# Reordering the start of a gated-recurrence and MLP kernel: later loads, the first transposed y on another queue, and a third unit begun in another order

## The chip, the cores and the metric

The kernel runs on one core of a Trainium2 chip. A core has five engines with an instruction stream each: TensorE (PE, matmuls and transposes), VectorE (DVE), ScalarE (ACT), GpSimd (POOL) and SyncE (SP), which here only issues DMAs. The metric is device time in microseconds, the median of several executions. Before the change it is 630.16 us (3 runs, 629.78 to 631.45).

## The reference

```python
f = 1.0 / (1.0 + np.exp(-f_logit))            # all of (4, 8, 768, 48)
for t in range(S):
    state = f[:, :, t, :, None] * state + np.einsum('bhd,bhe->bhde', k[:, :, t], v[:, :, t])
    y[:, :, t] = np.einsum('bhd,bhde->bhe', q[:, :, t], state)
x = y.transpose(0, 2, 1, 3).reshape(B * S, H * D)      # 3072 tokens, 384 columns
h = x @ w_in                                           # w_in 384 x 2048
g = h * (1.0 / (1.0 + np.exp(-1.702 * h)))
out = g @ w_out                                        # w_out 2048 x 384
```

A gated linear recurrence over 768 tokens for 4 batches and 8 heads, and behind it an MLP over all tokens. All data are float32.

## The kernel before

**Units.** The tokens are cut into 12 units of 256 (three for each batch). `attention(n)` builds one unit as a list of parts; each part is a function that issues instructions. The recurrence inside a chunk of 64 tokens is done by six levels (block sizes 1 to 32). At each level TensorE makes scores (`sc`, L392) from q and a copy of k set aside by ScalarE (`Kc`, L448; in units from the fourth on also a copy of q, `Qc`, L454). VectorE multiplies q and k by products of gates (`promote`: L473 in two halves for the first three units, L477 in one piece afterwards) and puts the scores into the matrix A under masks (L421, L441). After the levels, k is turned (`tkn`, copied to `kn`), A times v gives the inner part of y (L488), k times v the change of state (L576), and VectorE chains the four chunk states (L591 to L595, eight or seven short operations in a row). Then the states times q are added to y (L616), eight copies take y out of PSUM into `yT` (L627), and six DMAs bring `yT` into `xT`, where the MLP reads it (`to_x`, L648 and L653).

**Beginning a unit.** Three functions bring f, q and k of a unit into place: `begin_f`, `begin`, `begin_k`. In the first three units TensorE transposes them (L344) and ScalarE copies them out of PSUM (L349); from the fourth unit on VectorE does it (L332). f also passes a sigmoid on ScalarE, which must load another activation table before it and the table of the MLP's gelu after it. `begin_k` ends by setting k aside and, from the fourth unit on, by the first promotion. `begin_gates` makes the products of gates on GpSimd (L383). Each begin-function also issues the next unit's DMA load of the same input into the one `raw` buffer (`load_raw`).

**The MLP.** `mlp_blocks` (units 0 to 2, cut into four blocks of ff columns) and `mlp_unit` (the others) are lists of small TensorE steps: `h` (L784: three matmuls, then gelu on ScalarE, L788, into g) and `o` (L810; in later units seven products, L761). `merge` walks through a unit's attention parts and, after each, issues MLP steps in proportion to a share by the part's kind. So TensorE's order is written out by hand; it is the merged list. On the other engines a scheduler may move instructions. The weights come in 16 pieces of 768 KB (`fetch_weights`, L199, three buffers `bits`), and each is converted by one ScalarE operation (L217) and four VectorE operations (L219 to L222), dealt out among the parts by `convert`.

**Queues.** SP issues all loads and stores in one order[...].[...]

**The order around the change.** `parts_of(n)` puts the next unit's begin-functions among the parts of unit n. For n = 0: f and q between the late levels, k at the end. For n = 1: the third unit's q with the first part, its f before the last level but one, its k at the end. For n = 2 and 3: f, then q, then k, and after k the part with unit n's states. The inter-chunk y of unit n (L616) is issued with the first part of unit n + 1.

Of the kernel before, what the change touches and what calls it, by code (L numbers as in the profile page):

```python
# [16 lines left out]
def view(t, offset, dims):  # L17

    a = t[:]
    return bass.AP(a.tensor, a.offset + offset, [list(a.ap[0])] + [list(d) for d in dims])  # L20
# [3 lines left out]
def kernel(  # L24
# [33 lines left out]
    nc = tc.nc  # L58
    B, H, S, D = q.shape
# [10 lines left out]
    HS = 64  # L70
# [6 lines left out]
    N_FILL = 3  # L77
# [24 lines left out]
    def keep_up(times, columns=384, of=None):  # L102

        if times:
            pt = ps.tile([P, columns], F32, tag="mm", name=f"idle_{next(serial)}", bufs=4)
        for _ in range(times):
            lhs, rhs = of or (ident, masks.rearrange("p l f t -> p (l f t)"))
            nc.tensor.matmul(pt, lhsT=lhs, rhs=rhs, start=True, stop=True)  # L108
# [42 lines left out]
    def query(n, f):  # L151

        return ((2, 3), (4, 5) if n < N_FILL else (0, 5))[n % 2][f]

    q_end = const.tile([P, NP], F32, name="q_end")
# [14 lines left out]
    for r in range(NGR):  # L170
        ffs = range(r * FG, (r + 1) * FG)
        for ff in ffs[::2]:
            f = slice(ff * P, (ff + 2) * P)
# [126 lines left out]
    def rows(h):  # L300
        return slice(h * HS, h * HS + D)
# [4 lines left out]
    def attention(n):  # L306
# [10 lines left out]
        t = {"tms": [F]}  # L317
        parts = []

        def part(kind):  # L320
            return lambda fn: parts.append((kind, fn))

        def slot(s):
            return X[:, s]
# [31 lines left out]

        def begin_f():
            turn(0, lambda f: F[:, ORDER.index(f) * SLOT:(ORDER.index(f) + 1) * SLOT], AF.Sigmoid)
            if n:
                load_raw(n + 1, 0)  # L360

        def begin():
            turn(1, lambda f: slot(query(n, f)))
            if n:
                load_raw(n + 1, 1)

        def begin_k():
            turn(2, lambda f: slot((KR, KF)[f]))
            if n:
                load_raw(n + 1, 2)  # L370
            if n >= N_FILL:
                set_aside(0, True)
                promote(0)
            else:
                set_aside(0)
# [31 lines left out]
        def columns(h, g):  # L407

            return rows(h ^ g)
# [188 lines left out]
        @part("W")  # L598
        def _():

            py = t["py"]
            for cs in ((1, 0), (2, 3)):
                for a in range(NP):
                    for c in cs:
                        g, f = CHUNK[c]
                        w = HS
                        if t["before"][c] is None:
                            if not n:  # L610
                                continue
                            w = 1
                        for h in range(2):
                            state = t["before"][c][rows(h), a] if w > 1 else t["ahead"][rows(h), NC - 1, a]
                            x = a * HALF + g * HS
                            nc.tensor.matmul(  # L616
                                py[columns(h, g), g, a, f, :w], lhsT=state, rhs=X[rows(h), query(n, f), x:x + w],
                                start=False, stop=True, skip_group_check=True,
                            )
            yT = att.tile([P, NP, NG, G], F32, tag="kn", name=f"yT_{n}", bufs=1)  # L620
            xT = xTs[n] = mlp.tile([P, NK, width(n)], F32, tag="xT", name=f"xT_{n}", bufs=3)
            for f in (1, 0):
                for g in range(NG):
                    for h in range(2):
                        at, step = (g * HS, 1) if f else (U - 1 - g * HS, -1)
                        copy = nc.vector.tensor_copy if n == 0 and not f else nc.scalar.copy
                        copy(view(yT[rows(h)], at, [[U, NP], [step, HS]]), py[columns(h, g), g, :, f, :])  # L627
            to_x(lambda h: (yT[rows(h), :NK], lambda r, d: yT[r:r + d, NK]), xT[:, :, :U], NG)
            if n == NALL - 1:

                pl = ps.tile([P, NP], F32, tag="mm", name="y_last", bufs=4)
                for a in range(NP):
                    for h in range(2):
                        nc.tensor.matmul(
                            pl[rows(h), a:a + 1], lhsT=last["st"][rows(h), NC - 1, a], rhs=q_end[rows(h), a:a + 1],
                            start=True, stop=True,
                        )
                yl = att.tile([P, NP], F32, tag="q_last", name="yT_last", bufs=1)
                for h in range(2):
                    nc.scalar.copy(yl[rows(h)], pl[rows(h)])  # L640
                yl = yl.rearrange("p (a g t) -> p a g t", g=1, t=1)
                to_x(lambda h: (yl[rows(h), :NK], lambda r, d: yl[r:r + d, NK]), xT[:, :, U:], 1)

        def to_x(y, x, ng):

            for h in range(2):
                most, rest = y(h)
                nc.sync.dma_start(out=x[h * D:(h + 1) * D].rearrange("p c (g t) -> p c g t", g=ng), in_=most)  # L648
                at = 0
                while at < D:  # L650
                    c, p = (h * D + at) // DR, (h * D + at) % DR
                    w = min(D - at, DR - p)
                    nc.sync.dma_start(  # L653
                        out=x[D2 + p:D2 + p + w, c].rearrange("p (g t) -> p g t", g=ng), in_=rest(h * HS + at, w)
                    )
                    at += w
# [114 lines left out]
    def width(n):  # L771

        return U + (n == NALL - 1)
# [49 lines left out]
    def mlp_unit(n):  # L823
        g = {}

        def last_token():
            po = ps.tile([P, DM], F32, tag="mm", name="o_last", bufs=4)
            nc.tensor.matmul(po[:1], lhsT=ones, rhs=g["last"][:, 0], start=True, stop=True)
            nc.scalar.copy(g["last"][:1, 0], po[:1])
            nc.sync.dma_start(out=out[NALL * U - 1:, :], in_=g["last"][:1, 0])  # L830
        o = mlp_o7(n, g)
        if width(n) > U:
            o.insert(3 * HF, (DM, last_token, 0))
        return mlp_h(n, range(NFF), g, True) + o
# [28 lines left out]
    def parts_of(n):  # L863

        parts = list(units[n][1])
        _, inter = parts.pop()
        if n:
            kind, scores = parts[0]
            _, ahead = units[n - 1][1][-1]
            parts[0] = kind, lambda: (ahead(), scores())  # L870
        if n == 0:

            def and_idle(l):
                kind, fn = parts[l]
                return kind, lambda: (fn(), keep_up(2 * (l < 3)))
            parts[:NL] = [and_idle(l) for l in range(NL)]
        if n + 1 < NALL:
            begin_f, begin, begin_k, begin_gates = units[n + 1][0]
            i = len(parts)
            if n + 1 < N_FILL:  # L880

                parts.append(("K", lambda: (begin_k(), begin_gates())))
                parts.insert(i - 4, ("B", begin if n == 0 else lambda: None))
                parts.insert(i - 5, ("B", begin_f))
                if n:

                    kind, head = parts[0]
                    parts[0] = kind, lambda: (head(), begin(), keep_up(2 * (n == 1)))
                    if n == 1:
                        second = parts[1][1]  # L890
                        parts[1] = kind, lambda: (second(), keep_up(2))
            else:
                kind, states = parts.pop()
                if n in CARRY:
                    parts += [("B", begin_f), ("B2", begin), ("S1", lambda: (states(), begin_gates())), ("K3", begin_k)]
                else:
                    parts += [("B", begin), ("B", begin_k), (kind, lambda: (states(), begin_gates()))]
                    parts.insert(i - 3, ("B", begin_f))
        else:
            parts.append(("W", inter))  # L900
        return parts
# [58 lines left out]
    load_raw(1, 2)  # L960
    fetch_weights()
    fetch_weights()
    with nc.allow_non_contiguous_dma("one token"):
        for h in range(2):
            nc.sync.dma_start(out=q_end[h * HS:h * HS + D], in_=q[B - 1, h::2, S - 1, :].rearrange("a d -> d a"))
    fill = []
    merge(0, fill, 0, steady, deal=(0, 0, 0, 0, 0, 0, 0, 4, 1, 1, 0, 0))
    fill += mlp_blocks((0, 0)) + mlp_blocks((0, 1))
# [5 lines left out]
    fill_order.close()  # L974
    for n in range(3, NALL):
        fill += mlp_unit(n)
    for n in range(4, NALL):
        merge(n, fill, NFF * NK * U + 7 * HF * HC, late, chores=list(sums_of_b()) if n == 4 else ())
    for _, emit, _ in fill:
# [30 lines left out]
```

## Time and profile before

| | |
|---|---|
| median of 3 runs | 630.16 us |
| the profiled execution | 630.85 us |
| its span, first to last instruction | 629.0 us |
| TensorE busy | 603.4 us (96%) |
| VectorE busy | 385.4 us (61%) |
| ScalarE busy | 262.4 us (42%) |
| GpSimd busy | 42.3 us (7%) |
| mean DMA rate | 93 GB/s |

The page counts an engine as busy while an instruction runs. TensorE is busy nearly always, so the span is its work plus the time it waits; and its work takes longer where the granted clock (PEclk, tenths of full speed) is low. All of this lies in the first 240 us.

### The profile page before, as it was taken

To read this page: it belongs to the slowest core of one execution; us is meant where nothing else is said; L and a number is where in the kernel's file an instruction comes from. 1 tells how busy PE (TensorE), PEld (TensorE's weight loads), DVE (VectorE), ACT (ScalarE), POOL (GpSimd) and SP (SyncE) were. 2 spreads that over 40 slices of the span, in tenths; PEclk is the share of its full clock that TensorE was granted. 3 is DMA by queue.
4 is the path that set the end of the run, shared out by engine and by line. 5 is a ranking of instruction groups with operands and counts; after the bars stand their busy time and mean duration, and the time that the engine had idled before them with its cause. 6 is when DMAs were issued, how large, how long until landed. Compare 5 with 4: busy or idle time off the path is not lost.

```text
span 629.0 us, 17072 instructions
## 1 busy us (share of the span) xinstructions
PE 603.4 (96%) x7318; PEld 519.6 (83%) x7318; DVE 385.4 (61%) x632; ACT 262.4 (42%) x546; POOL 42.3 (7%) x91
## 2 busy tenths in 40 slices
PE   6888799889999999999999999999999999999997
PEld 5566577667678688989989989989989989989896
DVE  1788866678766656667657658646758646321441
ACT  3444554453155345345355355345345344232220
POOL 3010010020001002002002002002002001000000
PEclk9988799999999999999999999999999999999999
DMA  7857863372043451452553243543151111001000
GB/s 170 209 134 163 216 159 100 85 189 70 1 104 88 132 145 49 105 153 54 126 132 70 62 125 80 129 110 86 47 154 28 47 48 28 26 2 26 25 2 25
DMA packets 83308, 58.20 MB, mean 93 GB/s; under 512 B 33633, under 2 KB 75265, under 8 KB 83233
## 3 DMA queue, kind: packets, MB, share of 16 engines
q1 hardware_dynamic: 82480, 55.94, 35.6%
q10 hardware_dynamic: 753, 1.18, 0.8%
q8 instruction: 57, 0.93, 0.6%
q14 instruction: 18, 0.15, 0.1%
HBM read 43.98 MB, written 8.39 MB: 83 GB/s over the span
## 4 chain that ended last, share of the span: by engine, by line
PE 88%; ACT 3%; DVE 3%; DMA 2%; issue 2%; SPq 1%; ACTq 0%; DVEq 0%
PE h L784 37%; PE o L810 10%; PE o_Y L761 8%; PE o_Z L761 8%; PE o_X L761 7%; PE sc L392 6%; PE o_W L761 4%; PE t L344 2%; PE y L488 2%; PE sc L576 2%; PE y L616 2%; DMA raw<-in_f_logit_dram 1%; DMA bits<-in_moe_w_in_dram 1%; PE idle L108 1%; ACT yT L627 1%
## 5 line engine op out<-in xcount | busy, mean ns | idle before, releaser
L784 PE MATMUL h<-xT,w_in 128*128 128x256 f32 (+1 forms) x1152 | 258.6, 382 | 2.1 <-ACT g L788 2.1
L784 PEld LDWEIGHTS h<-xT,w_in 128*128 128x128 f32 x1152 | 217.5, 191 | 33.9 <-ACT g L788 2.7
L788 ACT ACTIVATE g<-h 128x256 f32<-128x256 f32 (+1 forms) x192 | 72.6, 385 | 199.1 <-PE h L784 198.7
L477 DVE TENSOR_TENSOR X<-X,tot 128x1024 f32<-128x1024 f32 x45 | 55.1, 1225 | 41.5 <-PE sc L392 35.2
L448 ACT COPY Kc<-X 128x512 f32<-128x512 f32 x72 | 48.0, 667 | 47.5 <-DVE X L477 24.7
L810 PE MATMUL o<-w_out,g 128*128 128x384 f32 x192 | 67.6, 503 | 0.0
L810 PEld LDWEIGHTS o<-w_out,g 128*128 128x128 f32 x192 | 36.3, 194 | 22.8 <-issue 1.2
L761 PE MATMUL o_Y<-T,S 128*128 128x192 f32 x288 | 51.7, 329 | 0.0
L441 DVE COPY_PREDICATED A<-masks,sc 128x256 f32<-128x256 uint32 (+1 forms) x108 | 51.0, 533 | 0.3
L761 PE MATMUL o_X<-w_out,g 128*128 128x192 f32 x288 | 49.7, 326 | 0.0
L761 PEld LDWEIGHTS o_Y<-T,S 128*128 128x128 f32 x288 | 47.0, 190 | 1.1 <-issue 0.7
L761 PEld LDWEIGHTS o_X<-w_out,g 128*128 128x128 f32 x288 | 47.5, 190 | 0.5
L383 POOL TENSOR_TENSOR tot<-F 128x512 f32<-128x512 f32 x12 | 12.5, 1041 | 473.7 <-DVE st L594 425.4
L392 PE MATMUL sc<-X,Kc 48*64 48x64 f32 x1440 | 31.2, 223 | 13.4 <-ACT Kc L448 7.3
L392 PEld LDWEIGHTS sc<-X,Kc 48*64 48x64 f32 x1440 | 26.4, 137 | 20.7 <-ACT Kc L448 10.3
L332 DVE STREAM_TRANSPOSE X<-raw 128x512 f32<-128x512 f32 x36 | 37.9, 1109 | 4.3 <-PE y L616 3.8
L627 ACT COPY yT<-y 48x256 f32<-48x256 f32 x92 | 33.7, 367 | 4.9 <-PE y L616 3.7
L699 DVE TENSOR_TENSOR g<-g,g 128x512 f32<-128x512 f32 x18 | 12.4, 691 | 37.3 <-ACT g L788 37.3
L473 DVE TENSOR_TENSOR X<-X,tot 128x512 f32<-128x512 f32 x30 | 20.2, 688 | 11.8 <-PE sc L392 11.8
L383 POOL TENSOR_TENSOR tot<-tot 128x256 f32<-128x256 f32 (+4 forms) x60 | 27.0, 449 | 4.7
L761 PE MATMUL o_Z<-w_out,g 128*128 128x192 f32 x144 | 26.7, 331 | 0.0
L697 DVE TENSOR_TENSOR S<-g 128x512 f32<-128x512 f32 x18 | 12.4, 692 | 21.7 <-ACT g L788 21.4
(93 smaller groups left out, 642.6 us busy)
## 6 DMA issues: line engine op xcount, KB each, us to landing
bits<-in_moe_w_out_dram SPq DMA_DIRECT2D x8, 768.0 KB, 7.0
raw<-in_f_logit_dram SPq DMA_DIRECT2D x48, 96.0 KB, 2.3
raw<-in_k_dram SPq DMA_DIRECT2D x48, 96.0 KB, 2.5
raw<-in_q_dram SPq DMA_DIRECT2D x44, 96.0 KB, 2.3
bits<-in_moe_w_in_dram SPq DMA_DIRECT2D x7, 576.0 KB
k_tok<-z SPq DMA_DIRECT2D x56, 64.0 KB, 1.8
kt<-k_tok SPq DMA_DIRECT2D x14, 256.0 KB, 2.9
xT<-yT SPq DMA_DIRECT2D x24, 144.0 KB, 2.7
```

Of the source, the lines that this page charges most:

```text
L332: nc.vector.transpose(view(out, at, [[HALF, NP], [step, R4], [R4 * step, 32]]), by_half[:, j, f].rearrange("p a (j d) -> p (a j) d", j=R4) ...
L383: nc.gpsimd.tensor_tensor(tn, t2[:, :, 0], t2[:, :, 1], ALU.mult)
L392: nc.tensor.matmul(t["sc"][g * HS:(g + 1) * HS, h, a, s, :], lhsT=t["Kc", l][rows(h), x:x + HS], rhs=rhs(h, a, g), start=True, stop=True,)
L441: nc.vector.copy_predicated(out=view(A, at, dims), mask=mask.bitcast(U32), data=got)
L448: nc.scalar.copy(c.rearrange("p (n two m) -> p n two m", two=2, m=m), view(X, KF * SLOT, [[2 * m, SLOT // (2 * m)], [(KR - KF) * SLOT + m, ...
L473: nc.vector.tensor_tensor(x, x, y, ALU.mult)
L477: nc.vector.tensor_tensor(x, x, y, ALU.mult)
L627: copy(view(yT[rows(h)], at, [[U, NP], [step, HS]]), py[columns(h, g), g, :, f, :])
L761: nc.tensor.matmul(t[bank], lhsT=lhs(f), rhs=rhs(f), start=(new and f == 0), stop=(f == HF - 1), skip_group_check=True,)
L784: nc.tensor.matmul(ph, lhsT=w_in[:, c, ff * P:(ff + 1) * P], rhs=xTs[n][:, c, :], start=(c == 0), stop=(c == NK - 1))
L788: nc.scalar.activation(g[ff // FG][:, ff % FG, :], ph, AF.Gelu_apprx_sigmoid)
L810: nc.tensor.matmul(t["po"], lhsT=g[ff // FG][:, ff % FG, tt * P:(tt + 1) * P], rhs=w_out[:, ff, :], start=(ff == ffs[0]), stop=(ff == ffs[ ...
```

## The change

- A load of the third unit (n = 2) is issued at other places: f in unit 1's `begin_f` as before, q with the first part of unit 1, k after the third unit's q has been turned. The three loads of the fourth unit are issued together, with the second part of unit 2, not in the third unit's begin-functions.
- The load of the last token's q (`q_end`) moves from the start to a later place in the source.
- The first unit's six `xT` DMAs are issued by ScalarE, not by SP. Its eight `yT` copies are shared by rows (heads: ScalarE the even, VectorE the odd), not by direction.
- In unit 1 the third unit's f is turned before level 2, ahead of the first gelu, and its q before level 4; two of the four filling matmuls (`keep_up`) go.
- In units 2 and 3 the states of unit n come before the next unit's `begin_k`; in unit 3 the next unit's q comes right after its f.

```diff
-            if n:
+            if n >= N_FILL or (n == 1 and 0 == 0):
                 load_raw(n + 1, 0)
...
-            if n:
+            if n >= N_FILL or (n == 1 and 1 == 0):
                 load_raw(n + 1, 1)
...
-            if n:
+            if n >= N_FILL or (n == 1 and 2 == 0):
                 load_raw(n + 1, 2)
...
-                        copy = nc.vector.tensor_copy if n == 0 and not f else nc.scalar.copy
+                        copy = nc.vector.tensor_copy if n == 0 and h else nc.scalar.copy
...
+            queue = nc.sync if n else nc.scalar
...
-                nc.sync.dma_start(out=x[h * D:(h + 1) * D].rearrange("p c (g t) -> p c g t", g=ng), in_=most)
+                queue.dma_start(out=x[h * D:(h + 1) * D].rearrange("p c (g t) -> p c g t", g=ng), in_=most)
...
-                parts.insert(i - 4, ("B", begin if n == 0 else lambda: None))
-                parts.insert(i - 5, ("B", begin_f))
-                if n:
+                if n == 0:
+                    parts.insert(i - 4, ("B", begin))
+                    parts.insert(i - 5, ("B", begin_f))
+                else:
                     kind, head = parts[0]
-                    parts[0] = kind, lambda: (head(), begin(), keep_up(2 * (n == 1)))
-                    if n == 1:
-                        second = parts[1][1]
-                        parts[1] = kind, lambda: (second(), keep_up(2))
+                    parts[0] = kind, lambda: (head(), load_raw(n + 1, 1), keep_up(2))
+                    parts.insert(4, ("B", lambda: (begin(), load_raw(n + 1, 2))))
+                    parts.insert(2, ("B", begin_f))
...
+                elif n < N_FILL:
+                    second = parts[1][1]
+                    parts[1] = parts[1][0], lambda: (second(), [load_raw(n + 1, j) for j in range(3)])
+                    parts += [("B", begin), (kind, lambda: (states(), begin_gates())), ("B", begin_k)]
+                    parts.insert(i - 3, ("B", begin_f))
                 else:
-                    parts += [("B", begin), ("B", begin_k), (kind, lambda: (states(), begin_gates()))]
-                    parts.insert(i - 3, ("B", begin_f))
+                    parts += [("B", begin_k), (kind, lambda: (states(), begin_gates()))]
+                    parts.insert(i - 3, ("B", lambda: (begin_f(), begin())))
...
-    with nc.allow_non_contiguous_dma("one token"):
-        for h in range(2):
-            nc.sync.dma_start(out=q_end[h * HS:h * HS + D], in_=q[B - 1, h::2, S - 1, :].rearrange("a d -> d a"))
     fill = []
...
     for n in range(3, NALL):
         fill += mlp_unit(n)
+    with nc.allow_non_contiguous_dma("one token"):
+        for h in range(2):
+            nc.sync.dma_start(out=q_end[h * HS:h * HS + D], in_=q[B - 1, h::2, S - 1, :].rearrange("a d -> d a"))
     for n in range(4, NALL):
```

More of the change, by code (lines that the diff above doesn't have):

```diff
@@ L652, in to_x @@
                     w = min(D - at, DR - p)
-                    nc.sync.dma_start(
+                    queue.dma_start(
                         out=x[D2 + p:D2 + p + w, c].rearrange("p (g t) -> p g t", g=ng), in_=rest(h * HS + at, w)
```

## The prediction

> **What bounds the kernel now.** I read first the page's engine totals and its row of the span in 40 slices, then busy time in stretches of 2 and 10 us, then the instructions in order of time around each hole, and last the built programs' order, for what each instruction waits for.
>
> ```profile
> PE   6888799889999999999999999999999999999997
> ...
> PEclk9988799999999999999999999999999999999999
> ```
>
> TensorE is busy 603.4 of 629.0 us; the other 25.6 us lie almost wholly in the first 140 us, and there the clock dips too. The change touches only units 0 to 3, so two stretches count. Columns below: stretch, its length, busy time and instructions of PE, weight load, DVE, ACT, POOL, then clock, DMA share, GB/s.
>
> ```profile
> 60.00:70.00 10.00, 4.97 (x42) 2.93 (x41) 7.23 (x13) 7.77 (x13) 0.00 (x0) 0.79 0.98 235
> ...
> 130.00:140.00 10.00, 7.83 (x267) 5.99 (x267) 8.99 (x14) 5.20 (x12) 4.18 (x5) 1.00 0.74 163
> ```
>
> The first hole, in order of time (idle time before, and what ended it, in brackets):
>
> ```profile
> 60.18 0.91 ACT L217 ACTIVATE a<-bits 128x768 f32<-128x768 f32 x1 [3.89 <-DMA bits<-in_moe_w_in_dram]
> ...
> 62.20 1.28 ACT L355 ACT_TABLE_LOAD   x1
> ...
> 64.56 1.28 ACT L788 ACT_TABLE_LOAD   x1
> ...
> 66.80 1.13 PE sc L392 x32
> ```
>
> A weight arrives at 60.1; behind it on ScalarE stand the third unit's f, two table loads and only then the last `Kc` of unit 1, for which TensorE waits 5.03 us (61.8 to 66.8). After that hole the clock is 0.50 from 66 to 72 us, and six `o` steps take 4.14 us where they take 1.94 later.
>
> The second hole, 130 to 137 us:
>
> ```profile
> 133.43 1.10 PE L616 MATMUL y<-X,st 48*48 48x64 f32 x36 [1.37 <-DVE st L595]
> 135.00 0.65 PE L616 MATMUL y<-X,st 48*48 48x64 f32 x28 [0.47 <-DVE st L595]
> ```
>
> TensorE waits for VectorE's chain of states. From its restart at 124.66 to the end of unit 3's first scores at 136.97 are 12.3 us with 9.5 us of work (h 5.37, y and states' products 2.03, y 1.04, scores 1.1), so 2.8 us of waiting.
>
> [...]
>
> **First stage, to 87 us. What is added.** The `yT` copies are shared, but the new program makes each wait for the one before on the other engine, so they don't overlap: 4 x 0.37 + 4 x 0.43 + 7 handoffs of 0.05 = 3.55, from 38.87 to 42.4 (before 42.07). Then ScalarE issues six DMAs. On SP they took 0.60, 0.61, 0.61, 0.52, 0.61, 0.61 (L648 and L653); ScalarE's own early issues took 0.3 to 0.7. The second, third and others wait for DMAs that landed before; the third for a 768 KB weight issued at 33.94, by the median 7.0 us landed at 40.9, by the longest 9.0 at 42.9, needed at 43.2; the sixth for the first, 2.7 us to land, 44.7. So from 41.95 to 45.75. Queued behind them is `Kc` of level 1: ready at 46.4 instead of 43.5, and TensorE is idle from 41.2 to 46.5. [...]TensorE has slack there.
>
> From there VectorE is the bound. With two X halves 1.29, copies into A 0.76 (level 1: 1.28), conversions 0.6, 0.6, 0.96, 0.96, a shuffle 0.6: level 1 with its scores 46.45 to 49.4, four conversions 52.5, level 2 54.5, shuffle and three conversions 57.2, level 3 59.25, three 61.4, level 4 63.45, three 65.95, level 5 67.95. Before: 69.98. **What is removed:** the wait for the weight (its load is no longer behind the fourth unit's q: issued at 45.5, not 53.2), and two of three table loads, 2.56 us of ScalarE, as f now stands ahead of the first gelu. `Kc` of level 3 waits for f and one table load till 54.95 and costs a hole of 1.85 us; no hole of 5. So TensorE keeps its clock and comes to y of unit 1 (L488) at 68.9, not 74.55.
>
> Then nine conversions (0.6, 0.96, 0.96, 0.6, 0.6, 0.96, 0.96, 0.6, 0.6 = 6.85) end at 74.8, eight state operations of 0.39 at 77.9; y and the next scores follow at 77.9 instead of 82.84. Copies of y (8 x 0.38) and `Kc` (0.69) give the level-1 scores at 81.45, before 86.71. **Gain 5.2 us.** If the last of the weights needed here, issued at 64.4, lands in 9 us and not 7, 0.8 less. The two dropped filling matmuls (0.75 us) lay in a hole: nothing. `q_end`'s two issues (0.95 us) leave SP at 21 us, where SP waits afterwards anyway: nothing; they come back after the third unit's k, needed 15 us later. The fourth unit's 28 load DMAs (some 0.5 us each on SP, 14 us) now run from 84 to 99 us, under dense TensorE work; the f among them is needed at 112, the weight behind them at 117: nothing. From 87 to 124 the orders are alike, and the table-load hole of 1.86 us before 124.66 stays.
>
> **Second stage, in before's times.** Unit 1's eleventh h moves behind the products of states (L576), and seven `o` steps (4.69 us) with it, as cover for the states. But the third `o` step needs a weight whose conversion stands on VectorE behind the states. Products end at 130.6; seven more operations of 0.39: 133.35; conversions 0.95 and 0.96, lengthened by about 0.9, since GpSimd's gates start at the same moment (before, L222 took 1.72 beside them): 136.15. TensorE is there at 133.2: 2.95 us of waiting. Next: y (L616) now waits for unit 4's first promotion, which the program puts ahead of it and whose slots it overlaps by the tracking of X. That stands behind L219 0.7, two k transposes 2.1, `Kc` and `Qc` 1.4 and itself 1.25: 141.7. TensorE is through its five `o` steps at 139.5: 2.2 us of waiting. Scores end at 143.85; work since 124.66 is 9.54 + 4.69 = 14.23 of 19.2 us, so 5.0 of waiting, 2.2 more than before. What is late next: y's copies to 145.8, six issues on SP to 149.1, landing 2.2: 150.7 for h of unit 2; TensorE is there at 149.9 (nine `o` steps), and the second h waits 0.35 for a sum. **Loss 2.6 us.** The move without its stalls would have gained up to 2.8[...].
>
> Units 3 and on: before has 0.22 us of waiting at 179; the new order has seven microseconds of `o` and h before the step that waits for the table loads: 0 to -0.2, taken as nothing.
>
> **Sum.** -5.2 + 2.6 = -2.6 us on the profiled execution (630.85, span 629.0): 628.25, span 626.4. The median shown is 0.7 below that execution, so 627.6.
>
> **Rivals.** (a) The second stage costs nothing: VectorE does the one conversion before the products of states end. For it: VectorE idles 126 to 130.6 there. Against: it stands behind the states in the program. -5.2 to -7: 623 to 625. (b) The second stage takes it all: halved clock after one of its two holes and late `xT`: +5, about 630. For: the earlier holes halved the clock. Against: at 120 to 124 a hole of 1.86 did not. (c) Slower: ScalarE's queue. If its six issues wait for landings (2.2 to 2.7 us each) and not for 0.6 us of issuing, `Kc` of level 1 is done at 54 or later, and VectorE's chain moves one for one: +7.5 against my sum, 635. The point: level-1 `Kc` ending 2.6 us later (49) is break-even, 4.5 later (51) measurably slower.[...] Against: SP issued the same six in 3.8 us. (d) It doesn't do what it says: the shared copies are that already, and are counted so.
>
> **How the numbers follow.** As worked 0.45 (own range 625 to 629.5), (a) 0.15, (b) 0.20, (c) 0.20. A measurement tells about 0.3%, 1.9 us: 628.3 and 632.1 are the bounds. Faster: (a) and three quarters of the first, 0.48; same: the rest of it and (b) but 0.03, 0.28; slower: (c) and a little of (b), 0.24. The range takes in (a)'s middle and the near half of (c): 623.5 to 633.5.
>
> **What would show it.** Right: `ACT_TABLE_LOAD` once, not three times, between 50 and 70 us; level-1 `Kc` at about 45.8; no PE hole over 2 us after 47; clock 1.00 from 60 to 75; level-1 scores of unit 2 near 81.5. Around 125 to 140 an `o` step (L811) waiting some 3 us for w_out's conversion, and y (L616) some 2 us for X L477. Wrong: `Kc` after 49, or neither of these two waits.

## The result, and the profile after

The changed kernel takes 629.87 us (median of 4 runs, 629.18 to 630.59); the kernel before, 630.11 us (4 runs, 629.78 to 631.45). The ratio is 0.9992, with a 95% interval of 0.9974 to 1.0011. So no difference can be measured. The profiled executions are 629.68 us (span 627.9) and 630.85 us (span 629.0): 1.2 us apart, of which most is the accident of which execution was profiled. TensorE is busy 602.8 us (before 603.4).

The page's TensorE row and clock row, of 40 slices of 15.7 us:

```profile
PE   7958999889999999999999999999999999999997
...
PEclk9898999989999999999999999999999999999999
```

The fifth slice of PE (63 to 78 us) is 9 where it was 7. The third (31 to 47 us) has become worse, 5 where it was 8, and in the ninth (126 to 141 us) the clock is 8 where it was 9. The same two stretches of 10 us as in the prediction, with the same columns:

```profile
60.00:70.00 10.00, 10.00 (x126) 6.57 (x129) 9.61 (x16) 6.18 (x13) 0.00 (x0) 1.00 0.63 192
...
130.00:140.00 10.00, 7.55 (x139) 4.77 (x140) 6.99 (x9) 3.21 (x6) 3.28 (x6) 0.83 0.56 153
```

From 60 to 70 us TensorE is now busy throughout at full clock (before: 4.97 us, clock 0.79). From 130 to 140 us it is busy a little less than before, and the clock fell to 0.83 (before: 1.00).

**First stage.** ScalarE's instructions of the changed kernel in order of time (start, duration, engine, line; in brackets the idle time before and what ended it). ACTq lines are DMAs that it issues:

```profile
41.74 0.60 ACTq L649 DMA_DIRECT2D xT<-yT  x1
...
44.64 2.47 ACTq L654 DMA_DIRECT2D xT<-yT  x2
47.16 0.67 ACT L448 COPY Kc<-X 128x512 f32<-128x512 f32 x1 [5.45 <-DMA raw<-in_q_dram]
```

In the kernel before, the same `Kc`:

```profile
42.83 0.68 ACT L448 COPY Kc<-X 128x512 f32<-128x512 f32 x1 [2.54 <-DVE X L473]
```

In the changed kernel it starts at 47.16, not at 42.83. The sixth DMA alone took 1.64 us to issue (45.48 to 47.11), where the five before it took 0.54 to 0.79. What held it isn't shown. The program gives the 526 DMAs of SP and ScalarE eight places (semaphores) between them, mostly in turn: by the traces the last holder of a place is the eighth DMA before in 504 of 518 cases, and in 484 of 518 after the change. Of 258 issues for which the landing of the last holder is told, five came while it was under way, and each of these started 0.02 us after it had landed. The sixth `xT` takes the place of the first, but that one had landed at 44.61. The bracket names a load of q as releaser; `Kc` starts 0.05 us after the sixth issue ends. TensorE, which waits for this `Kc` and comes back with a lowered clock (0.50 from 45 to 51 us), and later the restart of `h`, which is the end of the first stage, both of the changed kernel:

```profile
47.88 1.13 PE L392 MATMUL sc<-X,Kc 48*64 48x64 f32 x32 [6.71 <-ACT Kc L448]
...
120.42 4.15 PE L785 MATMUL h<-xT,w_in 128*128 128x256 f32 x18 [1.87 <-ACT g L789]
...
127.87 1.45 PE L811 MATMUL o<-w_out,g 128*128 128x384 f32 x4
132.29 5.19 PE L811 MATMUL o<-w_out,g 128*128 128x384 f32 x10 [2.96 <-DVE w_out L222]
137.64 1.11 PE L616 MATMUL y<-X,st 48*48 48x64 f32 x64 [0.17 <-DVE X L477]
...
146.23 5.95 PE L785 MATMUL h<-xT,w_in 128*128 128x256 f32 x26 [0.54 <-DMA xT<-yT]
```

The two ends of the second stage in the kernel before:

```profile
124.66 5.45 PE L784 MATMUL h<-xT,w_in 128*128 128x256 f32 x24 [1.86 <-ACT g L788]
...
147.40 1.46 PE L784 MATMUL h<-xT,w_in 128*128 128x256 f32 x6
```

The restart of `h` after the last table load is at 120.42, where it was at 124.66 before: 4.24 us gained between these two executions. Then the gain goes. **Second stage:** in both kernels TensorE does the same work from this restart to the first `h` after unit 3's first scores and 32 `o` matmuls: these, 24 `h` matmuls, the two products, y and the scores. Before, that was 124.66 to 147.40, 22.74 us. Now it is 120.42 to 146.23, 25.81 us: 3.07 us given back. Of the stage's length, 2.96 is the wait for `w_out`, 0.17 that for X, 0.54 that for `xT`; ten `o` matmuls took 5.19 us at the lowered clock (0.50 from 134 to 136 us), where at full clock 14 take 4.68 (in e5 below) and ten would take 3.34, so 1.85 are lost there; and the waits for `st` of the kernel before (1.37, 0.47, 0.22) are gone. The waits of the stage of before are therefore only exchanged for longer ones and for a slower clock.

### The profile page after: what moved, and what is told of

It reads as the page before. It is cut to its first block, busy times and chain, and to the rows that moved or that the text cites. A ratio compares the mean times of both kernels' runs of the same rounds, so it can differ in the third digit from the quotient of the medians.

```text
span 627.9 us, 17094 instructions
## 1 busy us (share of the span) xinstructions
PE 602.8 (96%) x7314; PEld 517.5 (82%) x7314; DVE 385.8 (61%) x632; ACT 260.3 (41%) x544; POOL 39.9 (6%) x91
## 4 chain that ended last, share of the span: by engine, by line
PE 87%; DVE 6%; ACT 3%; DMA 2%; issue 1%; SPq 1%; ACTq 0%; DVEq 0%
PE h L785 38%; PE o_X L762 8%; PE o_Y L762 8%; PE o L811 8%; PE o_Z L762 7%; PE sc L392 6%; PE o_W L762 4%; PE t L344 3%; PE y L616 2%; PE sc L576 2%; PE y L488 1%; PE idle L108 1%; DVE a L221 1%; DMA xT<-yT 1%; ACT yT L627 1%
## 5 line engine op out<-in xcount | busy, mean ns | idle before, releaser
L477 DVE TENSOR_TENSOR X<-X,tot 128x1024 f32<-128x1024 f32 x45 | 55.1, 1224 | 62.6 <-PE sc L392 49.4
L762 PE MATMUL o_X<-w_out,g 128*128 128x192 f32 x288 | 52.6, 331 | 0.0
L441 DVE COPY_PREDICATED A<-masks,sc 128x256 f32<-128x256 uint32 (+1 forms) x108 | 50.9, 534 | 0.1
L383 POOL TENSOR_TENSOR tot<-tot 128x256 f32<-128x256 f32 (+4 forms) x60 | 24.6, 410 | 4.7
L762 PE MATMUL o_W<-T,g 128*128 128x192 f32 x144 | 24.9, 326 | 0.0
L762 PE MATMUL o_Z<-w_out,g 128*128 128x192 f32 x144 | 24.9, 326 | 0.0
```

Of the source, the lines that this page charges most:

```text
L383: nc.gpsimd.tensor_tensor(tn, t2[:, :, 0], t2[:, :, 1], ALU.mult)
L441: nc.vector.copy_predicated(out=view(A, at, dims), mask=mask.bitcast(U32), data=got)
L477: nc.vector.tensor_tensor(x, x, y, ALU.mult)
L762: nc.tensor.matmul(t[bank], lhsT=lhs(f), rhs=rhs(f), start=(new and f == 0), stop=(f == HF - 1), skip_group_check=True,)
```

## The experiments

I took two theories into the first runs. One: the first stage gains 4.2 us, and the second gives back 3.0, because a weight conversion stands behind the states on VectorE. The rival: the lead is lost in any order, because data come when they come. Each ratio is to the kernel before, timed together with the run. "Restart" is the start of `h` after the hole (1.86 us before, 1.87 in the changed kernel) that an activation table load of 1.28 us leaves near 120 us; "stage two" runs from there to the `h` named above, with equal work in all.

| kernel | median, us | ratio to before | 95% interval | restart | stage two |
|---|---|---|---|---|---|
| before | 629.3 to 630.3 | 1 | | 124.66 | 22.74 |
| changed | 629.87 | 0.9992 | 0.9974 to 1.0011 | 120.42 | 25.81 |
| e1: k ahead of the states | 626.36 | 0.9950 | 0.9931 to 0.9969 | 120.14 | 22.74 |
| e2: xT on SP | 627.21 | 0.9962 | 0.9943 to 0.9981 | 116.97 | 25.81 |
| e3: before, states first | 631.71 | 1.0029 | 1.0009 to 1.0049 | 122.74 | 25.72 |
| e4: e1 and e2 | 623.86 | 0.9910 | 0.9889 to 0.9931 | 116.87 | 22.75 |
| e5: conversion ahead of the states | 628.27 | 0.9988 | 0.9974 to 1.0002 | 118.68 | 24.98 |
| e6: e5 and xT on SP | 626.73 | 0.9958 | 0.9943 to 0.9974 | 117.75 | 26.64 |
| e7: third unit's f at its old place | 629.26 | 0.9995 | 0.9979 to 1.0011 | 121.31 | 25.82 |
| e8: loads at their old places | 632.95 | 1.0060 | 1.0039 to 1.0082 | 123.08 | 25.79 |
| e9: before, fourth unit's loads later | 624.96 | 0.9915 | 0.9884 to 0.9947 | 116.44 | 22.74 |
| e10: e4, yT by direction | 625.06 | 0.9911 | 0.9881 to 0.9941 | 117.73 | 24.36 |
| e11: before, xT on ScalarE | 632.84 | 1.0044 | 1.0027 to 1.0060 | 127.20 | 22.74 |
| e12: e4, f at its old place | 625.35 | 0.9927 | 0.9903 to 0.9951 | 119.32 | 22.75 |

The last two columns come from one profiled execution each; with the same instructions up to there, the restart differs by up to 1.9 us between executions (124.66 before and 122.74 in e3; 120.42, 120.14 and 118.68 in the changed kernel, e1 and e5), while stage two repeats to a tenth, save where the clock differs. A difference of restarts below 2 us therefore shows little by itself. Microseconds below are the ratio less one, times 630.

### The second stage: e1, e3, e5

**e1**, the changed kernel with one part undone:

```diff
-                    parts += [("B", begin), (kind, lambda: (states(), begin_gates())), ("B", begin_k)]
+                    parts += [("B", begin), ("B", begin_k), (kind, lambda: (states(), begin_gates()))]
```

> The changed kernel, but in unit 2 the fourth unit's k is begun ahead of the states again, as before the change; the loads keep their new places. Theory (the first stage gains 4.2 us, and the second gives 3.0 of it back, because TensorE's third o step of the moved seven waits for a weight conversion behind the states): the 2.96 us wait of o (L811) near 132 us and the half clock after it go, the waits for the states of 1.4 and 0.5 us come back, and the 4.2 us stay: 4.0 to 4.5 us less than before, some 626 us. Rival (the lead of the first stage is lost in any order, since xT of unit 1 or a load comes when it comes): no more than 1.5 us less than before, and h of unit 2 waits 2 us or more for xT.

Measured: 3.2 us less than before (2.0 to 4.3 by the interval), median 626.36. The theory's 4.0 to 4.5 lies at the edge of the interval, the rival's 1.5 outside. As stage two of e1 is as long as that of before, these 3.2 us are also what the first stage gains by the timed runs; the 4.24 above came from one pair of executions. TensorE in order of time in e1:

```profile
120.14 5.45 PE L785 MATMUL h<-xT,w_in 128*128 128x256 f32 x24 [1.87 <-ACT g L789]
...
128.91 1.09 PE L616 MATMUL y<-X,st 48*48 48x64 f32 x36 [1.37 <-DVE st L595]
130.48 0.65 PE L616 MATMUL y<-X,st 48*48 48x64 f32 x28 [0.47 <-DVE st L595]
...
142.88 2.75 PE L785 MATMUL h<-xT,w_in 128*128 128x256 f32 x12
```

The wait of `o` is gone, the small waits for `st` are back, and the stage is 22.74 us again. Why the order matters is seen on VectorE. First the changed kernel, then e1, both up to the promotion (L477) of the fourth unit:

```profile
119.78 2.04 DVE L332 STREAM_TRANSPOSE X<-raw 128x512 f32<-128x512 f32 x2
121.67 0.34 DVE L594 TENSOR_TENSOR st<-st,tot 128x192 f32<-128x192 f32 x1
126.61 0.35 DVE L595 TENSOR_TENSOR st<-st,sc 128x192 f32<-128x192 f32 x1 [4.60 <-PE sc L576]
...
129.23 1.72 DVE L221 SCALAR_TENSOR_TENSOR a<-bits,a 128x768 f32<-128x768 uint32 x1
130.98 1.25 DVE L222 TENSOR_TENSOR w_out<-a,s 128x768 f32<-128x768 f32 x1
...
132.83 2.01 DVE L332 STREAM_TRANSPOSE X<-raw 128x512 f32<-128x512 f32 x2
136.36 1.23 DVE L477 TENSOR_TENSOR X<-X,F 128x1024 f32<-128x1024 f32 x1 [1.52 <-ACT Qc L454]
```

```profile
119.49 3.91 DVE L332 STREAM_TRANSPOSE X<-raw 128x512 f32<-128x512 f32 x4
126.04 1.23 DVE L477 TENSOR_TENSOR X<-X,F 128x1024 f32<-128x1024 f32 x1 [2.64 <-ACT Qc L454]
127.18 0.95 DVE L221 SCALAR_TENSOR_TENSOR a<-bits,a 128x768 f32<-128x768 uint32 x1
128.05 0.35 DVE L594 TENSOR_TENSOR st<-st,tot 128x192 f32<-128x192 f32 x1
```

States can't go on until TensorE's products (L576) are there, at 126.6. In e1 VectorE fills that time with the turning of k, the promotion and one conversion, and idles 2.64 us. In the changed kernel it idles 4.60 us with only the first state operation done, and k, promotion and both conversions come afterwards, when TensorE is waiting for them. The early place brings the states forward by 1.9 us only (their first L595 at 126.61, and at 128.50 in e1), since they wait in it for the products, and it puts everything else that TensorE is waiting for behind them.

**e3** does this part alone, in the kernel before, for unit 2 only:

```diff
-                    parts += [("B", begin), ("B", begin_k), (kind, lambda: (states(), begin_gates()))]
+                    if n == 2:
+                        parts += [("B", begin), (kind, lambda: (states(), begin_gates())), ("B", begin_k)]
+                    else:
+                        parts += [("B", begin), ("B", begin_k), (kind, lambda: (states(), begin_gates()))]
```

> The kernel before, with one part of the change: in unit 2 the states come before the fourth unit's k. Nothing of the first stage is changed. Theory (this part alone makes the loss): an o step waits some 3 us for w_out's conversion near 136 us, and the whole is 2.5 to 3.5 us slower than before. Rival (the stall arises only because the changed first stage brings TensorE there earlier than the weight): the wait is under 1 us, and the time within 1 us of before or, with the states' waits hidden, up to 2 us less.

Measured: 1.8 us slower (0.6 to 3.1). Its trace has the same line as the changed kernel's:

```profile
134.60 5.19 PE L810 MATMUL o<-w_out,g 128*128 128x384 f32 x10 [2.96 <-DVE w_out L222]
```

The wait is 2.96 us again, although TensorE comes there 2.3 us later: it isn't a matter of arriving early. Stage two is 25.72 us, 2.98 more than before. So this part loses about 3 us in its stage by itself; in the timed ratio only 1.8 show, with an interval that holds 3.

**e5** leaves the new order, and only takes the conversion out of the states' shadow (the numbers of VectorE operations dealt to the parts of unit 2, as they were worked out before, three of them moved up to the part that begins q):

```diff
-    merge(2, fill, UNIT + 3 * DM, steady, 10)
+    merge(2, fill, UNIT + 3 * DM, steady, 10, deal=(2, 2, 2, 3, 2, 2, 1, 1, 1, 3, 0, 1))
```

> The changed kernel, with one thing altered: the three VectorE operations of the weight conversion that the moved o steps wait for are dealt out one part earlier, ahead of unit 2's states and not behind them. Theory (the conversion's place behind the states is the whole cause of the second stage's loss; VectorE is idle for 4.6 us there): the 2.96 us wait of o goes, with the half clock after it, the moved o steps hide the states, and at most a wait of 1 to 2 us of y (L616) for the fourth unit's first promotion remains; 3.5 to 4.5 us less than the changed kernel, some 625.5. Rival (the moved steps are bad in themselves: the promotion's wait and the late xT take what the conversion frees): within 1.5 us of the changed kernel.

Measured: 0.9988, no measurable difference from the changed kernel's 0.9992. My theory in this form fell, and the rival stands. TensorE in e5:

```profile
126.13 4.68 PE L811 MATMUL o<-w_out,g 128*128 128x384 f32 x14
134.21 1.48 PE L616 MATMUL y<-X,st 48*48 48x64 f32 x64 [3.40 <-DVE X L477]
135.45 1.09 PE L392 MATMUL sc<-Qc,Kc 48*64 48x64 f32 x32
```

The `o` steps run through, and y waits 3.40 us for the promotion instead. On VectorE in e5 the conversion ends at 121.9 and the promotion still comes at 132.93, because k's transposes stand behind the states as before. The work after this hole is slow, as it was after the other (y and scores take 1.48 and 1.09 us, where 1.11 and 0.65 are usual). So the conversion was only the first in line. What costs is that everything VectorE owes TensorE here was put behind the states; e1, which takes k and the promotion back ahead of them, has neither wait.

### ScalarE's queue: e2, e4, e11

**e2**, the changed kernel with SP issuing the first unit's `xT`, and **e4**, with e1's edit too (shown is the edit of e2):

```diff
-            queue = nc.sync if n else nc.scalar
+            queue = nc.sync
```

> The changed kernel, but the first unit's xT DMAs are issued by SP again; the yT copies stay shared by rows. Theory (ScalarE's six issues, and the landing that the sixth waits for, hold Kc of level 1, and VectorE's chain of levels hangs on it): Kc of level 1 at 43 instead of 47.2, the 6.7 us hole of TensorE down to about 2.5, the half clock from 49 to 52 gone, and A of level 5 two to four microseconds earlier than 68.0; 1.5 to 4 us less than the changed kernel. Rival (from 50 us on VectorE waits for conversions and weights, not for Kc; the queue is hidden): A of level 5 within 0.7 us of 68.0, and the time within 0.7 us of the changed kernel.

> The changed kernel with both edits: k of the fourth unit ahead of unit 2's states, and the first unit's xT issued by SP. Theory (both effects are real and add, being in different stretches): 5.5 to 8 us less than before, some 622 to 624.5 us. Rivals: if the queue is hidden, as the kernel with k ahead of the states alone (about 626); if the second stage takes every lead, about 629.

Measured: e2 0.9962 against the changed kernel's 0.9992, about 1.9 us (0.2 to 3.6 by the two intervals). The restart is 3.45 us earlier in the profiled executions. e4 is 5.7 us less than before (4.3 to 7.0), and lies where the sum of two separate effects was expected. In e2 the scores behind level 1's `Kc` and the next y of unit 1:

```profile
43.52 1.13 PE L392 MATMUL sc<-X,Kc 48*64 48x64 f32 x32 [3.09 <-DVE A L421]
...
66.38 1.11 PE L488 MATMUL y<-A,vt 64*48 64x64 f32 x64
```

They start at 43.52, not 47.88, and 3.5 us of these 4.4 are still there at y (66.38, not 69.92). The queue isn't hidden: VectorE's chain of levels carries the delay (the copies into A of levels 1 and 5 start at 46.35 and 64.53, and at 49.69 and 68.00 in the changed kernel). Two marks were missed: TensorE's hole is 3.09 us and not 2.5, and the half clock isn't gone but comes earlier (0.50 from 44 to 46 us).

**e11** is that part alone in the kernel before: for the first unit the DMAs of L648 and L653 are issued by `nc.scalar`.

> The kernel before, with one part of the change: the first unit's six xT DMAs are issued by ScalarE. Theory (Kc of level 1 stands behind them, and VectorE's chain hangs on it): Kc of level 1 four microseconds later, and, since the late weight bounds the stretch here and takes up part of the delay, 1 to 3 us slower than before. Rival (the weight at 60 us bounds the stretch alone): within 0.7 us of before.

Measured: 2.8 us slower (1.7 to 3.8). `Kc` of level 1 starts at 46.20 instead of 42.83. The time is as expected, but the delay doesn't take the path of the theory. VectorE's copies into A (L441) of levels 1, 2 and 3 start 1.35 us late (48.31, 52.70, 57.17; before 46.97, 51.35, 55.82), those of levels 4 and 5 2.75 us late (66.15, 72.01; before 63.39, 69.26). Between them the weight comes in, on ScalarE in e11:

```profile
62.96 0.89 ACT L217 ACTIVATE a<-bits 128x768 f32<-128x768 f32 x1 [5.32 <-DMA bits<-in_moe_w_in_dram]
```

It came at 60.18 before. What held it is in the list of SP's waits of e11 between 30 and 66 us (total, times, longest):

```profile
SPq L291 <- DMA xT<-yT: 8.1, 1, 8.1
```

A load of v on SP (L291) waits there for the landing of an `xT` DMA, and ScalarE issues the first of these only at 41.84. So SP stood for 8.1 us with all that it had to issue behind that load, and the weight went out from 57.27 (before 53.19). In the kernel before, then, ScalarE's `xT` cost time by way of SP's order and the weight. That is the rival's mechanism, though not its size: the weight does bound the stretch, but it isn't fixed. In the changed kernel this weight is no longer what is waited for, and the delay goes through `Kc` and VectorE's chain (e2).

### Where the gain is: e8, e9, e7, e12, e10

**e8** gives the loads back to the begin-functions in the changed kernel, the third unit's too; **e9** moves the fourth unit's loads alone, in the kernel before (its edit, the other two begin-functions likewise):

```diff
-            if n:
+            if n and n != 2:
                 load_raw(n + 1, 0)
...
+                    if n == 2:
+                        second = parts[1][1]
+                        parts[1] = parts[1][0], lambda: (second(), [load_raw(n + 1, j) for j in range(3)])
```

> The changed kernel, but each begin-function issues the next unit's load again, as before the change; with q of the third unit now turned before level 4, the fourth unit's q is loaded from there. Theory (the later loads let a weight of 768 KB be issued 7.7 us sooner, and VectorE's conversions hang on it): ScalarE or VectorE wait 2 to 4 us for bits between 58 and 66 us, A of level 5 at 70 or later, and the whole is 1.5 to 4 us slower than the changed kernel. Rival (with f moved, the weights come in time in either order): within 1 us of the changed kernel.

> The kernel before, with one part of the change: the fourth unit's three loads are issued together in the second part of unit 2, not by the third unit's begin-functions. Order of f, q, k and states, xT, yT and the third unit's loads stay as before. Theory (the weight that stood behind the fourth unit's q is what the first stage waited for, and this part makes nearly the whole gain): ScalarE's wait of 3.89 us for bits near 60 us goes, TensorE's hole of 5 us before the last level's scores goes or halves, restart of h after the third table load 3 to 5 us earlier than 124.66, and the whole is 3 to 5 us less than before. Rival (VectorE's chain or the two table loads of the unmoved f take the weight's place): 1.5 us or less.

Measured: e8 is 3.8 us slower than before (2.5 to 5.2), some 4 more than the changed kernel. e9 is 5.4 us faster than before (3.3 to 7.3): this one part does all that the first stage was credited with, and no kernel here is measurably better. In e8, DMAs issued by SP, and what ScalarE then waits for:

```profile
66.66 1.86 SPq L267 DMA_DIRECT2D raw<-in_q_dram  x4
68.64 0.39 SPq L199 DMA_DIRECT2D bits<-in_moe_w_out_dram  x1
```

```profile
74.74 0.89 ACT L217 ACTIVATE a<-bits 128x768 f32<-128x768 f32 x1 [6.83 <-DMA bits<-in_moe_w_out_dram]
```

The fourth unit's q stands before a weight in SP's order, and ScalarE waits 6.83 us for that weight: not at 58 to 66 us, where I had expected it, but for a later weight, since q is turned later here. (A of level 5, expected at 70 or later, is at 65.94; the loss comes after it.) SP in the kernel before, and in e9:

```profile
51.23 1.86 SPq L267 DMA_DIRECT2D raw<-in_q_dram  x4
53.19 1.86 SPq L199 DMA_DIRECT2D bits<-in_moe_w_in_dram  x4
```

```profile
44.83 4.98 SPq L199 DMA_DIRECT2D bits<-in_moe_w_in_dram  x4
```

Before, the twelve DMAs of the fourth unit's q (from 45.55) go out ahead of the weight; without them it goes out 8.36 us sooner. ScalarE begins on it at 60.18 before, 7.0 us after its issue, and 7.0 is also the median of the weights from issue to landing; so it was late by its place in the order, and the transfer itself was no slower than usual. ScalarE in e9, in order of time, with the two table loads around f still there (1.28 us each, at 56.90 and 59.27):

```profile
55.69 1.19 ACT L349 ACTIVATE F<-t 128x256 f32<-128x256 f32 x4
...
60.84 0.61 ACT L448 COPY Kc<-X 128x512 f32<-128x512 f32 x1
```

f is turned 5.3 us earlier than in the kernel before (60.99 there), with no wait for bits, and the `Kc` behind the two loads costs TensorE a hole of 2.22 us where it was 5.03. The table loads still cost that hole, but no more. (The profiled execution of e9 is the fastest of its six and has the clock at 1.00 throughout, so its restart, 8.2 us earlier than before, overstates the gain; the timed runs give 5.4.)

**e7 and e12** turn the third unit's f behind the first gelus again, in the changed kernel and in e4:

```diff
-                    parts.insert(2, ("B", begin_f))
+                    parts.insert(6, ("B", begin_f))
```

> The changed kernel, but the third unit's f is turned where it was before the change, between the late levels of unit 1 and so behind the first gelus. Theory (f ahead of the first gelu saves two table loads and a hole of TensorE): three table loads again between 50 and 70 us, Kc of the last level behind two of them, a hole of TensorE of 2 to 4 us before 67 us; 2 to 3.5 us slower than the changed kernel, some 632 to 633. Rival (the later loads alone make the gain, since VectorE's chain and its weights bound the stretch): within 1 us of the changed kernel.

> The kernel with k ahead of the states and xT on SP (623.9 us), and the third unit's f turned at its old place, behind the first gelus. Theory (f's move is worth little: the table loads it saves lie in time that ScalarE has free): within 1 us of 623.9. Rival (its worth was hidden by the late Kc of level 1 alone): 2 us or more above it.

Measured: e7 0.9995 against 0.9992, e12 0.9927 against e4's 0.9910. Neither pair can be told apart; e12 may be up to 3 us slower. But the edit doesn't do what these expectations say. As q's part now stands ahead of level 4, `insert(6, ...)` puts f before level 5; in the kernel before it came before level 4. So the `Kc` of the last level, which stood behind f and two table loads there, goes ahead of them here (in e7 at 62.87, f's copies from 64.93), and the hole that I expected has no occasion to arise. The two runs show that f may come ahead of the first gelu or before level 5 with no measurable difference. Its old place wasn't run in the changed kernel. Nearest to it is e9, which has f at the old place, with the hole of 2.22 us, and is level with e4, which has f moved (0.9915, 0.9910). So f's move, in which I had seen half of the reason for the gain, is worth nothing that these runs can show; a worth of a microsecond or two isn't excluded.

**e10** divides the `yT` copies of e4 by direction again (`not f` in place of `h` in the choice of the engine).

> The kernel with k ahead of the states and xT on SP (623.9 us), and the first unit's yT copies shared by direction as before the change. Theory (the shared copies run one after another in either division, so the division is worth the 0.3 us by which they end): within 1 us of 623.9. Rival (copies by direction free ScalarE or VectorE sooner): 1.5 us or more below it.

Measured: 0.9911 against 0.9910. From the first copy to the following `Kc` are 4.05 us in e10 (38.91 to 42.96) and 4.14 in e4 (37.94 to 42.08). The division makes no difference that can be measured.

**e6** joins e5 and e2:

> The same, with the first unit's xT issued by SP as well. Theory (two separate stretches): 3.4 us less than the kernel with the earlier conversion alone, some 622; at least level with the kernel that begins k ahead of the states and issues xT on SP (623.9). Rival (with TensorE three microseconds earlier a weight or the promotion comes too late): no less than 624.5.

Measured: 626.73, the rival's side: 1.9 us less than e5, so the first stage gives what e2 gave, but y again waits 3.39 us for the promotion, and stage two is 26.64.

Together, each as it measured in the kernel before: loads -5.4 (e9), `xT` on ScalarE +2.8 (e11), states first +1.8 (e3; 3.0 by its stage), which makes -0.8; the whole change measured -0.5. The agreement is no closer than the intervals of one to two microseconds on each part, and the parts aren't quite independent: with the loads moved, `xT` on ScalarE costs 1.9 (e2), by another path. The third unit's loads and q, `q_end`, the filling matmuls and the order of unit 3 had no run of their own; e4, which has them all, and e9, which has none of them, are level, so that together they are worth no more than some 2.5 us either way. What e4 and e9 have in common, loads later, `xT` on SP, k ahead of the states, gives 0.991 of the time of before in both; that is the version to keep, and it beats both kernels.

## Why the prediction was right or wrong

It gave 627.6 us with a range of 623.5 to 633.5. The time, 629.87, lies in the range, 2.3 above the number given, and on the side of no change, to which I had given 0.28 against 0.48 for faster. The two halves had the right signs and the right places; each was somewhat off in the bad direction, and there was little left to lose. That the time fell in the range owes much to its width of 10 us: four fifths or more of the gain that was forecast isn't there.

- **"Gain 5.2 us", first stage.** Measured 4.24 (restart 120.42; also 4.24 at the level-1 scores, 82.47 for 86.71), and 3.2 by the timed runs (e1). The mis-sized term is ScalarE's six issues: "from 41.95 to 45.75" became 41.74 to 47.11. The sixth, which I had thought ready at 44.7 with the first landed, took 1.64 us by itself, though the first had landed at 44.61. `Kc` of level 1 started at 47.16, and not at about 45.8. From there the chain went as worked out: A of level 5 at 68.7 (67.95), y of unit 1 at 69.92 (68.9), unit 2's level-1 scores at 82.47 (81.45). Some 1.3 us late at its head, 1.0 at its end.
- **"TensorE has slack there."** TensorE may have it, but VectorE, which the next sentence called the bound, pays for the late `Kc`. I summed only the whole stage, and so never wrote down that this part alone costs time: 1.9 us in the changed kernel (e2). In the kernel before it costs 2.8 (e11), by a path that I didn't have at all: SP waits 8.1 us for a place that a DMA of ScalarE's holds. Rival (c) named the right queue, but the landing that it feared for the sixth issue had come 0.87 us before that issue began. The delay stayed below its break-even (47.8 for the end of `Kc`, where 49 was the point), so it took gain and didn't turn the sign.
- **"What is removed": the wait for the weight, and two table loads.** The first, done alone, gains as much as any kernel here (e9). A worth of the second isn't seen in any run, though f's old place was tried only without the rest of the change (e9), since e7 put f one level too late. I had put both into one chain, and so couldn't have known which carried it.
- **"2.95 us of waiting" of the third `o` step.** Measured 2.96, for the named conversion, lengthened beside GpSimd's products as supposed (L221 1.72 and L222 1.25, where 0.95 and 0.96 are usual; no run took GpSimd's work away).
- **"2.2 us of waiting" of y for the promotion.** Measured 0.17. The promotion was ready at 137.6, but the `o` steps before y ran 1.8 us too long on a lowered clock (0.50 from 134 to 136 us), and covered it. I had put that clock into rival (b) as one of its two conditions; here it came in place of the wait. e5 shows that the wait is real: with the `o` steps on time it is 3.40.
- **xT for `h` of unit 2, 0.8.** Measured 0.54.
- **"Loss 2.6 us."** Measured 3.07. The times beside it don't give 2.6: `h` of unit 2 at 150.7, which starts at 147.40 in the kernel before, is a loss of 3.3. Rival (b), the second stage taking all, was nearer than the likeliest case, by its halved clock (0.50 from 134 to 136 us); its +5 was my estimate.
- **Rival (a)**, the conversion before the products: tried as e5, and it doesn't make the stage free. The prediction had its reason for the promotion's wait in hand and didn't apply it to this rival.
- **"-5.2 + 2.6 = -2.6 us on the profiled execution".** Measured -1.2 between the two profiled executions: 4.24 less 3.07. The rest of the distance, to -0.24 in the medians, is that the profiled execution of before lies 0.7 above its median and that of after 0.2 below.

The marks set for "right" were met but for two: one table load between 50 and 70 us, no hole of TensorE over 2 us in that stage after the one that ends at 47.88, clock 1.00 from 60 to 75, an `o` step waiting 3 us; but `Kc` 1.4 us late, and no wait of y to speak of.

## What to carry to other kernels

A load issued early isn't free: it takes a place in its queue's order, and the one to look for is what the queue issues next and who waits for that; here moving 28 small loads, 12 of them right ahead of a weight, was worth 5.4 us, more than the whole change. In this program an issue moved to another engine's queue still shares the eight places with the first queue, and can hold it up there (8.1 us in e11). Before an operation is moved ahead of another on an engine, ask whether its own input is there: the states were put first and then waited 4.6 us for it, while the work that could have filled that time stood behind them, and mending only the first of the late pieces (e5) brought forward the next. When several parts are changed at once, price each by itself even where they share a stretch, since a sum that is right in size can hide a part that should be dropped.

## What the runs showed of the hardware that I had not expected

- Whether a hole lowers TensorE's clock isn't told by its length alone. The clock was 0.50 after holes of 2.07 us (kernel before, ahead of 48.40; from 49 to 52 us) and 2.96 us (changed kernel, ahead of 132.29; from 134 to 136 us), and after one of 3.40 us (e5) y and scores took 1.48 and 1.09 us, where 1.11 and 0.65 are usual; after 1.87 us ahead of `h` (changed kernel, from 120 to 124 us) the clock was 1.00. But e10 and e4 have the same three waits for `st` (1.36, 0.47, 0.22 in e10), and only e10 has the lowered clock after them. The stretch that follows in e10, then in e4:

```profile
130.00:135.00 5.00, 5.00 (x26) 2.88 (x20) 3.55 (x5) 2.92 (x7) 3.31 (x5) 0.69 0.84 223
```

```profile
130.00:135.00 5.00, 5.00 (x17) 2.99 (x16) 3.65 (x5) 2.09 (x5) 2.45 (x5) 1.00 0.89 229
```

  The clock, the third number from the end, is 0.69 and 1.00, and stage two is 24.36 and 22.75 us long. The same idle times can thus cost 1.6 us more or nothing. Why isn't shown: no run here moved a hole on purpose.
- Five of ScalarE's `xT` issues took 0.54 to 0.79 us and the sixth 1.64, though its place was free; a copy of 0.67 us (`Kc`) stood behind the six for 5.45 us. In the changed kernel SP waited 2.9 us, and in e11 8.1 us, for a place that one of ScalarE's DMAs held.
- A conversion step that starts with GpSimd's first and largest product of gates takes 1.72 us (L222 in the kernel before and in e1, L221 in the changed kernel), where it takes 0.95 alone; L222 right after it took 1.25. But not every overlap does this: beside the later, smaller products L221 and L222 took 0.94 and 0.96 (changed kernel, from 81.63).
